# Retention and a softplus MLP on one core: one PSUM group for scores, state and values, and three smaller moves

## The chip, the core and the metric

The kernel runs on one core of one Trainium2 chip. The metric is the device time of one execution in microseconds (us); lower is better. The engines are named as in the profile: PE is TensorE (PEld its weight loads), ACT is ScalarE, DVE is VectorE, POOL is GpSimd, SP is the engine that issues the DMAs. Each engine runs its own instructions in order, and they wait for one another by semaphores.

## The reference

For 8 batches, 8 heads, 576 positions and head size 64 the attention part is a retention: `scores = q k^T / 8`, multiplied by a decay `gamma_h ** (i - j)` for `i >= j` and 0 above the diagonal, times `v`. Its output, 4608 tokens by 512, goes through an MLP:

```python
h = x @ w_in                                            # 512 -> 2048
g = np.maximum(h, 0.0) + np.log1p(np.exp(-np.abs(h)))   # softplus
return (g @ w_out).astype(np.float32)                   # 2048 -> 512
```

## The kernel before

**Attention.** The tokens are cut into 36 chunks of 128. A chunk's scores are masked, and what came before the chunk enters through a running state (one per batch and head) that is scaled on POOL. The first nine chunks run in plain fp32, two head pairs at once: a *double step* m (18 of them) handles half of a chunk. `scores_double` writes the scores and the new state of a double step into two PSUM banks (columns 0 to 3C of them, C = 128), `scores_double_out` masks the scores on DVE (two instructions, L176) and adds up the state (L185 or L187), `values_double` multiplies the masked scores and the earlier state into another pair of banks, and `values_double_out` brings the result into the MLP's input: a copy on ACT (L216) and the rounding remainder on DVE (L217). The other 27 chunks run in split fp32r steps, which the change does not touch.

**MLP.** 512 tokens are a unit u (9 units), 128 of the 2048 hidden features a part p (16). A *slot* i is one pair (u, p), 144 in all: `hidden_mm(i)` (L380, 12 matmuls of 512 columns, every operand split into a high and a low half), then on ACT three functions (`logs`, L389 to L391), on DVE the sum (`softplus`, L395), on ACT the cast of the high half and on DVE the low half (`softplus_split`, L399, L400), then `output_mm` (L413, 12 matmuls). On PE slot i runs `hidden_mm(i)` and then `output_mm(i - 1)`, so that the softplus of a slot has about one slot of time.

**Stages.** An opening runs the first nine double steps (m = 0 to 8, AHEAD = 9). Slots 0 to 18 (SPLIT = 19) then carry the other nine (m = 9 to 17), and in the same slots the MLP's weights are loaded and split, two pieces of 512 KB a slot, by `weight_step`, once at the head of the slot and once behind `softplus_split`: ACT `weight_a` (L443) and `weight_c` (L459), DVE half of `weight_a` (L445), `weight_d` (L464) and `weight_b` (L451), and the load of the piece two ahead, which waits until `weight_d` has freed a buffer. Before the change odd slots hold `scores_double(m)` and even slots `values_double(m)`:

```python
            if i % 2:
                scores_double(m, two_banks(2))
                scores_double_out(m)
                scale_next()
            else:
                values_double(m, two_banks(2))
                values_double_out(m)
                if i:
                    load_next()
            weight_step()
```

The order of instructions on every engine is that of the program; nothing reorders them. A tile's slot in a pool is handed on when all its readers are done. At the end of each unit `output_out` copies four results from PSUM (by turns ACT, L422, and DVE, L424) and stores them. PSUM holds four banks for y as two tiles of two banks each, two for the double steps, two that serve the opening and then h. The last slot takes its softplus in two halves of 256 columns.

Of the kernel before, what the change touches and what calls it, by code (L numbers as in the profile page):

```python
# [36 lines left out]
PIECE = 512  # L37
START_WEIGHTS = 3
# [21 lines left out]
def retention_softplus_ffn(ctx: ExitStack, tc, opening, first, others, w, dec, vsc, gchp, out):  # L60
# [7 lines left out]
    ps_y = ctx.enter_context(tc.tile_pool(name="ps_y", bufs=1, space=PSUM))  # L68
# [123 lines left out]
    def values_double(m, bank):  # L192
        L = live[-1 - m]
        start, _ = _chunk_kind(m // 2)
        n_cross = C if start is None else start
        if L["before"] is None:
            n_cross = 0
        for s in range(2):
            for h in range(2):
                rows = slice(h * D, (h + 1) * D)  # L200
                nc.tensor.matmul(bank[rows, s, 0:C], L["v"][:, s, rows], L["a"][:, h, s], start=True,  # L201
                                 stop=not n_cross, skip_group_check=True)
        if n_cross:
            for s in range(2):
                for h in range(2):
                    rows = slice(h * D, (h + 1) * D)
                    nc.tensor.matmul(bank[rows, s, 0:n_cross], L["before"][rows, s], L["q"][rows, s, 0:n_cross],  # L207
                                     start=False, stop=True, skip_group_check=True)
        L["o"] = bank

    def values_double_out(m):
        o = live.pop(-1 - m)["o"][:, :, 0:C]
        ch, pr = m // 2, 2 * (m % 2)
        xt = x_tile(ch // CPU)
        cols = slice((ch % CPU) * C, (ch % CPU + 1) * C)
        nc.scalar.copy(xt[:, HI, pr:pr + 2, cols], o)  # L216
        nc.vector.tensor_sub(xt[:, LO, pr:pr + 2, cols], o, xt[:, HI, pr:pr + 2, cols].bitcast(F32))  # L217
# [151 lines left out]
    hs = {}  # L369
# [3 lines left out]
    def hidden_mm(i):  # L373
        u, p = divmod(i, NF)
        xt = x_tile(u)
        h = later["ps_h"].tile([P, T], F32, tag="h", name="h")
        n = 0
        for a, b in TERMS:
            for kt in range(NKT):
                nc.tensor.matmul(h, ws[p][:, a, kt * P:(kt + 1) * P], xt[:, b, kt],  # L380
                                 start=(n == 0), stop=(n == 3 * NKT - 1))
                n += 1
        hs[i] = h

    def logs(i, cols=slice(0, T)):

        h = hs[i][:, cols]
# [6 lines left out]
    def softplus(i, ab, cols=slice(0, T)):  # L394
        nc.vector.scalar_tensor_tensor(ab, hs[i][:, cols], 0.0, ab, op0=ALU.max, op1=ALU.add)  # L395
# [7 lines left out]
    def output_mm(i):  # L403
        u, p = divmod(i, NF)
        parts = gs.pop(i)
        if p == 0:
            ys[u] = [ps_y.tile([P, 2, DM], F32, tag=f"y{n}", name=f"y{n}") for n in range(2)]
        for tt in range(CPU):
            y = ys[u][tt // 2][:, tt % 2]
            for n, (a, b) in enumerate(TERMS):  # L410
                g = parts[tt * len(parts) // CPU]
                at = tt % (CPU // len(parts)) * P
                nc.tensor.matmul(y, g[:, a, at:at + P], ws[p][:, b, PIECE:],  # L413
                                 start=(p == 0 and n == 0), stop=(p == NF - 1 and n == 2))

    def output_out(u, tt):

        y = ys[u][tt // 2][:, tt % 2]
        pool = later.get("osb", moe) if tt > 1 else moe
        osb = pool.tile([P, DM], F32, tag="osb", name="osb")  # L420
        if tt % 2 == 0:
# [60 lines left out]
    load_weight(0)  # L482
    for m in range(6):
        load_double(m)
    load_weight(1)
# [13 lines left out]
    def two_banks(n):  # L499
        pool, tag = ((ps_y, "y0"), (ps_y, "y1"), (ps_att, "bank"), (ps_open, "open"))[n]  # L500
# [8 lines left out]
    weight_a(0)  # L509
    weight_b(0)  # L510
    weight_c(0)
    weight_d(0)
    scale_values(0)
    for m in range(AHEAD):
# [9 lines left out]
        if m in (2, 4, 6):  # L524
            load_weight(m // 2 + 1)
        scale_values(m + 1)
        scores_double_out(m)
        if m in (4, 6):
            weight_b(m // 2 - 1)
        if m in (5, 7):  # L530
            weight_d(m // 2 - 1)
        if 0 < m < AHEAD - 1:
            values_double_out(m - 1)
        if m in (4, 6):
            weight_c(m // 2 - 1)
        if m in (3, 5):
            weight_a(m // 2)
        scale_next()
    wpos[0] = START_WEIGHTS
    open_pools.close()  # L540
    later["ps_h"] = ctx.enter_context(tc.tile_pool(name="ps_h", bufs=2, space=PSUM, side="right"))

# [3 lines left out]
    for i in range(NSLOT):  # L546
        j = i + LEAD
        if i < SPLIT:
            m = AHEAD + (i - 1) // 2
            if i % 2:  # L550
                scores_double(m, two_banks(2))
                scores_double_out(m)
                scale_next()
                if "raw" in later:
                    load_upto(NPLAIN + 1)
            else:
                values_double(m, two_banks(2))
                values_double_out(m)
                if i:
                    load_next()  # L560
# [34 lines left out]
        hidden_mm(i)  # L595
        ab = logs(i)
        if i < SPLIT:
            softplus(i, ab)
# [7 lines left out]
        if i >= SPLIT:  # L606
            softplus(i, ab)
# [9 lines left out]


    hidden_mm(i)
    halves = [slice(0, T // 2), slice(T // 2, T)]  # L620
    abs_ = [logs(i, cols) for cols in halves]
    output_mm(i - 1)
    gs[i] = []
    for ab, cols in zip(abs_, halves):
        softplus(i, ab, cols)
        gs[i].append(softplus_split(ab))
    output_mm(i)
    for tt in range(CPU):
        output_out(NUNIT - 1, tt)
# [53 lines left out]
```

## Time and profile before

| | us |
|---|---|
| median of 3 runs (lowest, highest) | 956.22 (955.93, 958.87) |
| the profiled execution | 956.29 |
| its span, first to last instruction | 954.6 |
| busy in the span: PE, ACT, DVE, POOL | 943.3, 674.6, 668.8, 280.0 |
| granted PE clock, mean | 0.999 of full speed |

The span is what the trace shows; the profiled execution's own time is 1.7 us longer, for what lies before and after it. PE is busy for 99% of the span, and the chain of work that ended last consists of PE for 96%. A row of the timeline gives start, duration, engine, source line, operation, the tile written and the tile read, and in square brackets the idle time of the engine ahead of it and what ended that. A row of the chain gives start, duration and what the chain was on; its pieces add up to the span.

### The profile page before, as it was taken

How to read it: one execution, taken by the hardware profiler on the slowest of the kernel's cores; microseconds unless marked ns; L12 is line 12 of the kernel's file. 1: busy time of each engine (PE TensorE's matmuls, PEld its weight loads, DVE VectorE, ACT ScalarE, POOL GpSimd, SP SyncE). 2: the span in 40 equal slices, each digit the busy share in tenths (PEclk: the TensorE clock that was granted, in tenths of full speed). 3: DMA queues.
4: the chain of work that ended last, by engine and by line, in shares of the span. 5: the costliest groups of instructions: out<-in, count | busy, mean ns of one | idle time of the engine just before them, and what ended most of it. 6: DMA issues, size and time to landing. Idle time of an engine off the chain costs nothing.

```text
span 954.6 us, 14474 instructions
## 1 busy us (share of the span) xinstructions
PE 943.3 (99%) x4934; PEld 788.5 (83%) x4934; DVE 668.8 (70%) x1507; ACT 674.6 (71%) x1449; POOL 280.0 (29%) x497
## 2 busy tenths in 40 slices
PE   7999999999999999999999999999999999999997
PEld 6777777888888888888888888888888888888886
DVE  6688855777877777777777787778777787753222
ACT  6677756777777777777777777777777777764443
POOL 5222112333343332333343333233333333200000
PEclk9999999999999999999999999999999999999999
DMA  8556623212312232213212222223212222201001
GB/s 316 180 162 214 196 92 105 65 52 67 98 63 67 59 102 67 67 51 99 78 50 67 67 94 67 67 56 105 67 52 64 78 85 66 67 1 45 1 1 44
DMA packets 28729, 79.85 MB, mean 84 GB/s; under 512 B 3440, under 2 KB 3440, under 8 KB 28656
## 3 DMA queue, kind: packets, MB, share of 16 engines
q1 hardware_dynamic: 28656, 78.93, 26.1%
q8 instruction: 39, 0.64, 0.3%
q14 instruction: 34, 0.28, 0.1%
HBM read 69.48 MB, written 9.44 MB: 83 GB/s over the span
## 4 chain that ended last, share of the span: by engine, by line
PE 96%; DMA 2%; ACT 1%; DVE 1%; POOL 0%; issue 0%; SPq 0%; POOLq 0%; ACTq 0%; DVEq 0%
PE h L380 41%; PE y L413 40%; PE os L348 7%; PE sc L266 3%; PE os L275 2%; DMA raw_rawp<-first 1%; PE bank L201 1%; PE bank L161 1%; PE bank L207 1%; DMA out<-osb 0%; PE bank L166 0%; DVE a L176 0%; ACT ab L390 0%; ACT ab L391 0%; ACT ab L389 0%; ACT osb L422 0%
## 5 line engine op out<-in xcount | busy, mean ns | idle before, releaser
L380 PE MATMUL h<-xt,w 128*128 128x512 f32 x1728 | 420.4, 392 | 0.0
L413 PE MATMUL y<-w,g 128*128 128x512 f32 x1728 | 415.8, 389 | 0.8 <-DVE g L400 0.8
L413 PEld LDWEIGHTS y<-w,g 128*128 128x128 f32 x1728 | 324.0, 188 | 69.6 <-DVE g L400 1.9
L380 PEld LDWEIGHTS h<-xt,w 128*128 128x128 f32 x1728 | 316.0, 188 | 62.6 <-issue 1.0
L241 POOL TENSOR_TENSOR raw<-raw,dec_sb 128x256 f32<-128x256 f32 x108 | 98.0, 908 | 436.3 <-DMA raw<-others 361.3
L400 DVE TENSOR_TENSOR g<-ab,g 128x512 fp32r<-128x512 f32 (+1 forms) x145 | 103.9, 716 | 98.8 <-ACT g L399 98.8
L399 ACT CAST g<-ab 128x512 fp32r<-128x512 f32 (+1 forms) x145 | 89.5, 617 | 114.4 <-DVE ab L395 114.4
L395 DVE SCALAR_TENSOR_TENSOR ab<-h,ab 128x512 f32<-128x512 f32 (+1 forms) x145 | 99.6, 687 | 82.4 <-ACT ab L391 76.6
L389 ACT ACTIVATE ab<-h 128x512 f32<-128x512 f32 (+1 forms) x145 | 86.2, 594 | 64.9 <-PE h L380 64.7
L391 ACT ACTIVATE ab<-ab 128x512 f32<-128x512 f32 (+1 forms) x145 | 91.3, 629 | 4.6
L390 ACT ACTIVATE ab<-ab 128x512 f32<-128x512 f32 (+1 forms) x145 | 91.2, 629 | 4.6
L255 ACT CAST hl<-raw 128x768 fp32r<-128x768 f32 x108 | 90.9, 841 | 1.7 <-POOL raw L246 1.7
L257 DVE TENSOR_TENSOR hl<-raw,hl 128x512 fp32r<-128x512 f32 x108 | 84.8, 785 | 1.5
L285 DVE TENSOR_TENSOR a<-sc,a 128x256 f32<-128x256 f32 x108 | 45.8, 424 | 55.9 <-ACT a L284 55.0
L361 ACT CAST xt<-os 64x128 fp32r<-64x128 f32 x216 | 56.3, 261 | 36.3 <-PE os L275 31.9
L348 PE MATMUL os<-ah,hl 128*128 128x256 f32 x324 | 73.3, 286 | 0.0
L365 DVE TENSOR_TENSOR xt<-os,xt 64x128 fp32r<-64x128 f32 x216 | 62.2, 288 | 2.8
L309 POOL TENSOR_TENSOR s<-s,gchp_sb 128x128 f32<-128x128 f32 x96 | 58.6, 611 | 9.2 <-DVE s L308 0.2
L317 ACT CAST ah<-a 128x256 fp32r<-128x256 f32 x108 | 44.0, 407 | 15.1 <-POOL a L286 10.9
L348 PEld LDWEIGHTS os<-ah,hl 128*128 128x128 f32 x324 | 53.6, 190 | 0.4
L286 POOL TENSOR_SCALAR_AFFINE_SELECT a<-a 128x256 f32<-128x256 f32 x108 | 44.9, 416 | 29.4 <-DVE a L285 28.5
L256 DVE TENSOR_TENSOR hl<-raw,hl 64x256 fp32r<-64x256 f32 x108 | 47.4, 439 | 8.5 <-ACT hl L255 5.5
(82 smaller groups left out, 786.5 us busy)
## 6 DMA issues: line engine op xcount, KB each, us to landing
raw<-others SPq DMA_DIRECT2D x108, 384.0 KB, 3.1
wst<-w SPq DMA_DIRECT2D x32, 512.0 KB, 3.7
out<-osb SPq DMA_DIRECT2D x36, 256.0 KB, 2.2
raw_rawp<-first SPq DMA_DIRECT2D x13, 512.0 KB, 4.6
raw_g<-first SPq DMA_DIRECT2D x3, 512.0 KB, 7.4
raw_ab<-first SPq DMA_DIRECT2D x2, 256.0 KB, 8.5
dec_sb<-dec SPq DMA_DIRECT2D x1, 512.0 KB, 3.9
part<-opening SPq DMA_DIRECT2D x1, 390.0 KB, 4.3
```

The source lines that it names most:

```text
L241: nc.gpsimd.tensor_mul(r[:, 2:4], r[:, 2:4], later["dec"][:, 2 * pr:2 * pr + 2])
L255: nc.scalar.copy(hl[:, 0:6], r)
L257: nc.vector.tensor_sub(hl[:, 6:10], r[:, 2:6], hl[:, 2:6].bitcast(F32))
L348: nc.tensor.matmul(o[:, :, 0:width], lhs, rhs, start=(n == 0), stop=(n == len(mms) - 1))
L380: nc.tensor.matmul(h, ws[p][:, a, kt * P:(kt + 1) * P], xt[:, b, kt], start=(n == 0), stop=(n == 3 * NKT - 1))
L389: nc.scalar.activation(ab, h, AF.Abs)
L390: nc.scalar.activation(ab, ab, AF.Exp, scale=-1.0)
L391: nc.scalar.activation(ab, ab, AF.Ln, bias=1.0)
L395: nc.vector.scalar_tensor_tensor(ab, hs[i][:, cols], 0.0, ab, op0=ALU.max, op1=ALU.add)
L399: nc.scalar.copy(g[:, HI], ab)
L400: nc.vector.tensor_sub(g[:, LO], ab, g[:, HI].bitcast(F32))
L413: nc.tensor.matmul(y, g[:, a, at:at + P], ws[p][:, b, PIECE:], start=(p == 0 and n == 0), stop=(p == NF - 1 and n == 2))
```

## The change

- In slots 1 to 17 the odd slot runs `scores_double(m)` and `values_double(m - 1)` one behind the other into the same two banks (the values in columns 3C to 4C, `VCOLS`), and both outputs behind them. The even slots have no attention any more, but for slot 18, which holds the last values. The load of the next double step moves to the odd slot, directly ahead of the scaling on POOL.
- The first piece of the weights is loaded behind the second double step instead of ahead of everything, and its conversion moves from ahead of the opening into it; the other pieces' steps shift by one or two iterations.
- The y tiles become four of one bank each, opened behind the opening; the opening's six banks are a pool of their own.
- At the end of unit 0 two of the four results are staged in the opening's input tiles `part0` and `part1` (free since the first double step) instead of two buffers shared with the masked scores.
- In the last slot `hidden_mm` is computed in two halves of 256 columns into two h tiles, and of the last four results the last is copied by ACT instead of DVE.

The core of the diff (left out are only the changed arguments of `logs` and `softplus`, which take the tile h instead of its number):

```diff
+VCOLS = slice(3 * C, 4 * C)
...
-    ps_y = ctx.enter_context(tc.tile_pool(name="ps_y", bufs=1, space=PSUM))
...
     def values_double(m, bank):
...
-                nc.tensor.matmul(bank[rows, s, 0:C], L["v"][:, s, rows], L["a"][:, h, s], start=True,
+                nc.tensor.matmul(bank[rows, s, VCOLS], L["v"][:, s, rows], L["a"][:, h, s], start=True,
...
     def values_double_out(m):
-        o = live.pop(-1 - m)["o"][:, :, 0:C]
+        o = live.pop(-1 - m)["o"][:, :, VCOLS]
...
-    def hidden_mm(i):
+    def hidden_mm(i, cols=slice(0, T)):
...
-                nc.tensor.matmul(h, ws[p][:, a, kt * P:(kt + 1) * P], xt[:, b, kt],
+                nc.tensor.matmul(h, ws[p][:, a, kt * P:(kt + 1) * P], xt[:, b, kt, cols],
...
     def output_mm(i):
-            ys[u] = [ps_y.tile([P, 2, DM], F32, tag=f"y{n}", name=f"y{n}") for n in range(2)]
+            ys[u] = [later["ps_y"].tile([P, DM], F32, tag=f"y{n}", name=f"y{n}") for n in range(CPU)]
...
-    def output_out(u, tt):
-        y = ys[u][tt // 2][:, tt % 2]
-        pool = later.get("osb", moe) if tt > 1 else moe
-        osb = pool.tile([P, DM], F32, tag="osb", name="osb")
-        if tt % 2 == 0:
+    def output_out(u, tt, last=0):
+        y = ys[u][tt]
+        if u == 0 and tt > 1:
+            osb = parts[tt - 2][:, 0:DM]
+        else:
+            osb = (later["osb"] if tt > 1 else moe).tile([P, DM], F32, tag="osb", name="osb")
+        if tt % 2 == last:
...
-    load_weight(0)
     for m in range(6):
         load_double(m)
-    load_weight(1)
+        if m in (2, 5):
+            load_weight(m // 3)
...
-        pool, tag = ((ps_y, "y0"), (ps_y, "y1"), (ps_att, "bank"), (ps_open, "open"))[n]
+        pool, tag = ((ps_open, "open0"), (ps_open, "open1"), (ps_att, "bank"), (ps_open, "open2"))[n]
...
-    weight_a(0)
-    weight_b(0)
-    weight_c(0)
-    weight_d(0)
     scale_values(0)
     for m in range(AHEAD):
...
-        if m in (2, 4, 6):
-            load_weight(m // 2 + 1)
+        if m in (3, 5, 7):
+            load_weight((m + 1) // 2)
         scale_values(m + 1)
         scores_double_out(m)
-        if m in (4, 6):
+        if m in (2, 4, 7):
             weight_b(m // 2 - 1)
-        if m in (5, 7):
-            weight_d(m // 2 - 1)
+        if m in (3, 5):
+            weight_d((m - 3) // 2)
         if 0 < m < AHEAD - 1:
             values_double_out(m - 1)
-        if m in (4, 6):
+        if m in (2, 4, 7):
             weight_c(m // 2 - 1)
-        if m in (3, 5):
-            weight_a(m // 2)
+        if m in (1, 3, 6):
+            weight_a(m // 3)
         scale_next()
+    weight_d(START_WEIGHTS - 1)
...
             if i % 2:
-                scores_double(m, two_banks(2))
+                bank = two_banks(2)
+                scores_double(m, bank)
+                values_double(m - 1, bank)
                 scores_double_out(m)
+                values_double_out(m - 1)
+                if i > 1:
+                    load_next()
                 scale_next()
...
-            else:
+            elif i == SPLIT - 1:
                 values_double(m, two_banks(2))
                 values_double_out(m)
-                if i:
-                    load_next()
             weight_step()
...
-    hidden_mm(i)
-    halves = [slice(0, T // 2), slice(T // 2, T)]
-    abs_ = [logs(i, cols) for cols in halves]
+    hs = [hidden_mm(i, slice(n, n + T // 2)) for n in (0, T // 2)]
+    abs_ = [logs(h) for h in hs]
...
-        output_out(NUNIT - 1, tt)
+        output_out(NUNIT - 1, tt, last=1)
```

## Rows read from the trace of the kernel before

**Rows 1.** Timeline of the opening: start, duration, engine, line, operation, out<-in, [idle <-releaser].
```profile
11.05 1.06 ACT L153 ACTIVATE raw_g<-raw_g,part 128x64 f32<-128x64 f32 x4
11.76 0.73 POOL L137 TENSOR_TENSOR raw_g<-raw_g,part 128x256 f32<-128x256 f32 x1
...
21.38 0.71 PE L161 MATMUL bank<-raw_rawp 64*128 64x128 f32 x8 [0.56 <-POOL raw_rawp L137]
```
**Rows 2.** Chain of waits, end of the opening and first slots: start, duration, what.
```profile
22.48 0.44 PE bank L201 x8
...
25.32 0.43 PE bank L166 x8
...
27.61 2.96 PE h L380 x12
...
32.55 0.70 DVE ab L395
...
34.73 3.06 PE y L413 x12
```
**Rows 3.** Chain of waits, slots 7 and 8, the pattern of slots 1 to 16.
```profile
75.57 2.72 PE y L413 x12
78.29 0.59 PE bank L201 x8
78.88 0.58 PE bank L207 x8
79.46 2.95 PE h L380 x12
...
85.13 0.65 PE bank L161 x8
```
**Rows 4.** Timeline of DVE and of ACT in the same slots, the loop's marks.
```profile
72.70 0.69 DVE L395 SCALAR_TENSOR_TENSOR ab<-h,ab 128x512 f32<-128x512 f32 x1 [0.52 <-ACT ab L391]
...
77.09 0.28 DVE L185 TENSOR_TENSOR s<-bank,s 128x128 f32<-128x128 f32 x1
...
79.56 0.68 DVE L395 SCALAR_TENSOR_TENSOR ab<-h,ab 128x512 f32<-128x512 f32 x1
...
81.93 0.36 ACT L216 CAST xt<-bank 128x256 fp32r<-128x256 f32 x1
82.21 0.68 ACT L443 ACTIVATE wst<-wst 128x512 f32<-128x512 f32 x1
83.39 0.68 ACT L459 CAST w<-wst 128x512 fp32r<-128x512 f32 x1 [0.49 <-DVE wst L451]
...
85.91 0.69 DVE L395 SCALAR_TENSOR_TENSOR ab<-h,ab 128x512 f32<-128x512 f32 x1 [0.52 <-ACT ab L391]
```
**Rows 5.** One line's instructions in 40 to 130 us; durations in ns, minimum/median/maximum.
```profile
L451 DVE SCALAR_TENSOR_TENSOR wst<-wst x26: 680/686/1224, 42.1 to 126.0; 128x512 int32<-128x512 int32 x26
```
**Rows 6.** Loads of double steps (tile raw_rawp) in 40 to 130 us, from issue.
```profile
DMA to landing us min/median/max: 4.4/4.6/5.1
```
**Rows 7.** Timeline of DVE at the end of unit 0.
```profile
145.13 0.76 DVE L176 TENSOR_TENSOR a<-bank,mask 128x256 f32<-128x256 f32 x2 [1.13 <-DMA out<-osb]
```
**Rows 8.** Chain of waits, slots 18 to 20.
```profile
147.28 2.94 PE h L380 x12
...
152.94 0.23 PE sc L266 x2
...
153.41 2.75 PE h L380 x12
```
**Rows 9.** Timeline of the last 10 us.
```profile
944.99 0.42 DVE L395 SCALAR_TENSOR_TENSOR ab<-h,ab 128x256 f32<-128x256 f32 x1 [3.00 <-ACT ab L389]
...
946.67 3.05 PE L413 MATMUL y<-w,g 128*128 128x512 f32 x12 [0.58 <-DVE g L400]
...
948.99 0.69 DVE L424 COPY osb<-y 128x512 f32<-128x512 f32 x1 [1.08 <-ACT osb L422]
...
950.38 0.69 DVE L424 COPY osb<-y 128x512 f32<-128x512 f32 x1 [0.70 <-ACT osb L422]
```

More of the change, by code (lines that the diff above doesn't have):

```diff
@@ L206, in values_double @@
                     rows = slice(h * D, (h + 1) * D)
-                    nc.tensor.matmul(bank[rows, s, 0:n_cross], L["before"][rows, s], L["q"][rows, s, 0:n_cross],
+                    nc.tensor.matmul(bank[rows, s, 3 * C:3 * C + n_cross], L["before"][rows, s], L["q"][rows, s, 0:n_cross],
                                      start=False, stop=True, skip_group_check=True)
@@ L366, in value_out @@
         return rest
-    hs = {}
     gs = {}
     ys = {}
-    def hidden_mm(i):
+    def hidden_mm(i, cols=slice(0, T)):
         u, p = divmod(i, NF)
         xt = x_tile(u)
-        h = later["ps_h"].tile([P, T], F32, tag="h", name="h")
+        h = later["ps_h"].tile([P, T], F32, tag="h", name="h")[:, cols]
         n = 0
@@ L379, in hidden_mm, with logs @@
             for kt in range(NKT):
-                nc.tensor.matmul(h, ws[p][:, a, kt * P:(kt + 1) * P], xt[:, b, kt],
+                nc.tensor.matmul(h, ws[p][:, a, kt * P:(kt + 1) * P], xt[:, b, kt, cols],
                                  start=(n == 0), stop=(n == 3 * NKT - 1))
                 n += 1
-        hs[i] = h
-    def logs(i, cols=slice(0, T)):
-        h = hs[i][:, cols]
+        return h
+    def logs(h):
         ab = moe.tile([P, h.shape[1]], F32, tag="ab", name="ab")
@@ L392, in logs, with softplus @@
         return ab
-    def softplus(i, ab, cols=slice(0, T)):
-        nc.vector.scalar_tensor_tensor(ab, hs[i][:, cols], 0.0, ab, op0=ALU.max, op1=ALU.add)
+    def softplus(h, ab):
+        nc.vector.scalar_tensor_tensor(ab, h, 0.0, ab, op0=ALU.max, op1=ALU.add)
     def softplus_split(ab):
@@ L414, in output_mm @@
                                  start=(p == 0 and n == 0), stop=(p == NF - 1 and n == 2))
-    def output_out(u, tt):
-        y = ys[u][tt // 2][:, tt % 2]
-        pool = later.get("osb", moe) if tt > 1 else moe
-        osb = pool.tile([P, DM], F32, tag="osb", name="osb")
-        if tt % 2 == 0:
+    def output_out(u, tt, last=0):
+        y = ys[u][tt]
+        if u == 0 and tt > 1:
[3 more added lines that the diff above has]
+        if tt % 2 == last:
             nc.scalar.copy(osb, y)
@@ L541, in retention_softplus_ffn @@
     later["ps_h"] = ctx.enter_context(tc.tile_pool(name="ps_h", bufs=2, space=PSUM, side="right"))
+    later["ps_y"] = ctx.enter_context(tc.tile_pool(name="ps_y", bufs=1, space=PSUM, side="right"))
     SPLIT = NPLAIN - LEAD
@@ L594, in retention_softplus_ffn @@
             break
-        hidden_mm(i)
-        ab = logs(i)
+        h = hidden_mm(i)
+        ab = logs(h)
         if i < SPLIT:
-            softplus(i, ab)
+            softplus(h, ab)
             gs[i] = [softplus_split(ab)]
@@ L606, in retention_softplus_ffn @@
         if i >= SPLIT:
-            softplus(i, ab)
+            softplus(h, ab)
             if ends:
@@ L616, in retention_softplus_ffn @@
             output_out(i // NF - 1, 3)
-    hidden_mm(i)
-    halves = [slice(0, T // 2), slice(T // 2, T)]
-    abs_ = [logs(i, cols) for cols in halves]
+    hs = [hidden_mm(i, slice(n, n + T // 2)) for n in (0, T // 2)]
+    abs_ = [logs(h) for h in hs]
     output_mm(i - 1)
     gs[i] = []
-    for ab, cols in zip(abs_, halves):
-        softplus(i, ab, cols)
+    for h, ab in zip(hs, abs_):
+        softplus(h, ab)
         gs[i].append(softplus_split(ab))
```

## The prediction, made before the changed kernel ran

> **What bounds the kernel now.** I read the chain of waits first. In slots 1 to 16 it is PE alone, piece behind piece: 2.72 us of output matmuls, 0.59 and 0.58 for the values, 2.95 hidden matmuls, and in the next slot 0.65 for the scores [rows 3]. With 0.43 for a state [rows 2] two slots take 0.59 + 0.58 + 0.65 + 0.43 + 2 x (2.95 + 2.72) = 13.59 us. From slot 20 on a hidden group that doesn't follow fp32 attention takes 2.75 [rows 8].
>
> PE alone says little about what comes next, so I read the timelines of ACT and DVE in the same slots. Call S(i) the start of softplus(i) on DVE; 34.73 - 32.55 = 2.18 us after it PE may start the output matmuls of slot i [rows 2]. S runs 72.70, 79.56, 85.91 for slots 6, 7, 8: 6.86 us from even to odd, 6.35 from odd to even, 13.21 a pair [rows 4]. None of these softplus waits for PE: two wait for ACT's functions, the third comes straight behind other DVE work. Weight conversion and softplus are thus a loop of ACT and DVE with its own pace, only 0.38 us a pair faster than PE. Whatever makes PE faster there meets this loop at once, and what lengthens it by more than 0.38 slows the kernel.
>
> **The slots on PE.** The merged block is 0.65 + 0.43 + 0.44 + 0.58 = 2.10 us; the 0.44 is a values group behind a state group [rows 2]. The even slot's hidden group then follows output matmuls and takes 2.75. A pair needs 2.10 + 2.95 + 2.72 + 2.75 + 2.72 = 13.24 us, 0.35 less than now.
>
> **The slots on ACT and DVE.** The same instructions run, but the copy of the values (L216) now stands in the odd slot behind `scores_double_out`, and it reads the very two banks that DVE's masks and state read. What do two engines do that read one PSUM tile? Rows 9 show it twice, at the end of the kernel. A softplus half starts at 944.99 and was released by ACT's read of the other half of its h tile, not by its own input. DVE's copy at 948.99 waited 1.08 us for ACT's copy out of the same y tile. So readers of one tile take turns in program order, even at other columns. In both cases ACT is first; the change needs the other order, which no row shows. The Trainium skill (PSUM — Partial Sum Buffer, section PSUM bank collisions raise a hardware error) says that software must order any two engines on one bank and the same partitions, two reads included, whichever comes first. By that rule the copy waits for DVE's state instruction, as I take it below; without such an order the time is that of the second rival.
>
> Price of this wait. In slot 7 the state ends at 77.09 + 0.28 = 77.37 [rows 4]. ACT is strict in order: behind the copy stand `weight_a`, `weight_c` and the three softplus functions. The copy's record lasts 0.36 us and the next instruction starts 0.28 behind its start, so I count `weight_a` (0.68) as 0.60; from `weight_c` to softplus it is 85.91 - 83.39 = 2.52 [rows 4]. 77.37 + 0.28 + 0.60 + 2.52 = 80.77, that is 8.07 us behind S(6), where it is 6.86 now. From odd to even the copy's absence gives nothing: `weight_c` waits 0.49 us for DVE there anyway [rows 4], so 6.35 stays. A pair of the loop takes 14.42 us. I take 14.5, because the scaling on POOL now runs beside the odd softplus chain: an instruction such as L451 takes 0.69 us alone and up to 1.22 beside POOL [rows 5]. Two such in the chain make at most 2 x 0.54; little of it seems likely, since POOL has 0.73 us an instruction alone [rows 1] and falls partly on other work. Bounds: 14.2 (the masks and state begin a little sooner) and 15.5. PE with its 13.24 then idles about 1.2 us a pair.
>
> **The moved load.** The load of a double step goes from the even slot to the odd one; on SP it stays between the two weight loads, and its buffer was freed by PE long before. POOL's scaling now stands directly behind it and waits for it. It is issued before the state instruction at the latest, lands 5.1 us later at most [rows 6], which is 77.09 + 5.1 - 80.77 = 1.4 us behind the odd softplus, and two scalings of 0.73 [rows 1], 1.2 at worst, end 3.8 behind it. PE wants them with the next odd block, 2.18 + 2.72 = 4.9 behind it. On POOL only the next odd slot's state is queued behind. So no cost; if the cover of 1.1 us went, the scores would wait.
>
> **The opening.** Three pieces bring the first hidden group forward from 27.61 [rows 2]. The values of double step 8 no longer stand before it: 27.61 - 25.75 = 1.86 us, 25.75 being the end of the last state group [rows 2]. The fourth double step's data were there by 11.05, when ACT used them without waiting, but POOL scaled them at 11.76, held up by a chain that starts with the second double step's load [rows 1]; with 512 KB less ahead of that load the 0.71 goes. PE's wait of 0.56 at 21.38 for a later load [rows 1] goes too, as the third weight piece is now queued behind that load. The weight conversion that moves into the opening (three DVE and two ACT instructions) lies under PE's fp32 work; if it did not, DVE's part costs up to 3 x 0.69. Bounds of the three pieces: 1.86 and 3.7. I take 3.13: hidden(0) at 24.48, S(0) 4.94 later [rows 2] at 29.42.
>
> **The sum to slot 18.** S(1) = 29.42 + 8.07 = 37.49, PE being ahead of it or catching up within a pair. S(13) = 37.49 + 6 x 14.5 = 124.49, and the output matmuls of slot 13 start at 126.67. Behind slot 14 the weights are done and PE is the bound again. To hidden(18) it still has 2.72; slot 15 with 0.65 + 0.44 + 0.58 = 1.67 (no state in the last chunk) + 2.95 + 2.72; slot 16 with 2.75 + 2.72; slot 17 with 1.67 + 2.95 + 2.72; and 1.17 of values: 24.04. So hidden(18) starts at 150.71 instead of 147.28 [rows 8]: 3.43 us later. At the end of unit 0 DVE's wait of 1.13 us for a store [rows 7] goes with the extra staging tiles. A new one comes: the second staging copy takes the buffer of masked scores that PE reads in slot 17, 1.67 us on; behind it on DVE stand one more copy and the masks, and PE needs them only after its hidden group of 2.95. That hides it.
>
> **Slots 19 to 142** are fp32r attention and the MLP; nothing in them changes but the size of the y tiles, for which PE does not wait. I count nothing.
>
> **The tail.** The last hidden group becomes 24 matmuls of 256 columns at 0.23 / 2 us [rows 8], 2.76 us instead of 2.75, and its first half is ready 1.38 us sooner. So PE's 0.58 us wait for g [rows 9] goes (0 to 0.58). Behind PE's end at 946.67 + 3.05 = 949.72 two copies stand in a row now, to 951.07, because they share a y tile [rows 9]; with one tile each only one of at most 0.69 + 0.03 is left: 0.63 less. Together 1.2 us.
>
> **Sum.** 3.43 - 1.2 = +2.2 us on the profiled execution's 956.29, which is 0.07 above the median of the runs: **958.5 us**. A change of 0.3%, 2.9 us, is about what a measurement of this kernel can tell from none.
>
> **Rivals.**
> - *POOL beside the loop* (slower). If the scaling on POOL falls on L400, L464 and L451 of the odd chain, a pair grows by one or two times 0.54. Above 14.6 us a pair the kernel is more than 0.3% slower; at 14.96 it is 958.5 + 6 x 0.46 = 961.3, at 15.5 it is 964.5. For it: such durations occur now, under `weight_d` and `weight_b` of the odd slot [rows 5]. Against: POOL's work then meets fewer such instructions. [...]
> - *The copy doesn't wait for DVE's reads* (faster). Even to odd is then 6.86 plus 0.36 for the remainder at most, a pair at most 13.6 and more likely PE's 13.24. S(1) is at 36.6, six pairs of 13.3 lead to 126.67 - 8.1 = 118.6, hidden(18) is at 142.6, 4.7 earlier than before, and the time 956.29 - 4.7 - 1.2 = 950.4. For it: no row shows DVE first and ACT second. Against it are the two cases of rows 9.
> - *The opening doesn't move* but for the 1.86: 1.3 later, 959.8. That the dropped DMA piece isn't what delays it is the case here.
>
> **How the numbers follow.** Forecast 62%, of which a seventh lies above +0.3%; POOL beside the loop 20%; copy without a wait 9%; the opening stuck 9%. Faster by over 0.3%: 9%. Slower: 62 / 7 = 9, plus 20, plus 6 of the last: 35%. Within: 56%. The range is that of the forecast with its bounds, 14.2 us a pair and a better opening below (958.5 - 1.8 - 0.6 = 956.1), the POOL rival at its middle above, and a little of the others: 955.8 to 961.6.
>
> **What would show it.** In the changed trace: ACT's L216 released by DVE's L185 in the odd slots; softplus 8.1 and 6.35 us apart by turns; PE idle about 1.2 us a pair ahead of L413 (by L400) or L380 (by L464); hidden(0) near 24.5 and hidden(18) near 150.7; no idle PE ahead of the last L413. Wrong would be a pair of 13.3 us or of 15 and more.

## The result and the profile after

The changed kernel takes 960.64 us (median of 7 runs, 960.02 to 961.30) beside 956.74 (955.91 to 958.87) for the kernel before on the same chip: a ratio of 1.0032, with a 95% interval of 1.0021 to 1.0042. It is slower, by about the bound of 0.3%. The seven times of the kernel before fall into two groups, 955.9 to 956.7 and 958.2 to 958.9 us (see the last section): the change costs 4 to 5 us beside the first and about 2 beside the second. The profiled execution took 960.02 us with a span of 958.3, against 956.29 and 954.6 before. In the page's chain of work that ended last PE's share falls from 96% to 87%; ACT has 7% and DVE 5% now.

**The loop of ACT and DVE.** Timeline of DVE and ACT in the slots 6 to 8; the columns are those of [rows 4], and two lines that stood there come back here in their new order.

```profile
74.33 0.69 DVE L394 SCALAR_TENSOR_TENSOR ab<-h,ab 128x512 f32<-128x512 f32 x1 [0.53 <-ACT ab L390]
...
78.72 0.28 DVE L185 TENSOR_TENSOR s<-bank,s 128x128 f32<-128x128 f32 x1
...
79.09 0.37 ACT L216 CAST xt<-bank 128x256 fp32r<-128x256 f32 x1 [2.28 <-DVE s L185]
...
82.45 0.69 DVE L394 SCALAR_TENSOR_TENSOR ab<-h,ab 128x512 f32<-128x512 f32 x1 [0.53 <-ACT ab L390]
...
88.80 0.69 DVE L394 SCALAR_TENSOR_TENSOR ab<-h,ab 128x512 f32<-128x512 f32 x1 [0.52 <-ACT ab L390]
```

ACT is ready for the copy of the values (L216) 2.28 us before it runs, and it runs when DVE has read the state out of the same two banks (78.72 + 0.28 = 79.00). Softplus now runs 8.12 and 6.35 us apart by turns, where [rows 4] have 6.86 and 6.35. From S(1) = 38.96 to S(13) = 125.90 six pairs take 86.94 us, 14.49 each. The view of waits (ACT, 30 to 140 us; columns: total us, times, longest) shows the same wait at every copy:

```profile
ACT xt L216 <- DVE s L185: 13.7, 6, 2.3
...
ACT xt L216 <- DVE s L187: 2.3, 1, 2.3
ACT xt L216 <- DVE a L176: 1.5, 1, 1.5
```

**The end of the opening.** Timeline of PE, to be read beside [rows 2]:

```profile
23.53 0.71 PE L161 MATMUL bank<-raw_g 64*128 64x128 f32 x8
24.17 0.45 PE L166 MATMUL bank<-raw_g 128*64 128x64 f32 x8
25.80 2.98 PE L380 MATMUL h<-xt,w 128*128 128x512 f32 x12 [1.17 <-DVE s L187]
```

The values of double step 8 are gone from here, but the first hidden group waits 1.17 us for DVE's state instruction of that double step. In the chain the work between the output matmuls of slot 13 and hidden(18), which was at 147.28 before [rows 8], reads:

```profile
128.18 3.02 PE y L412 x12
...
131.84 0.59 PE bank L201 x8
...
144.76 0.59 PE bank L201 x8
...
152.77 2.95 PE h L380 x12
```

**The tail.** Timeline of the last 10 us, to be read beside [rows 9]: the last two output groups (24 matmuls) now follow one another without the wait of 0.58 us, and one copy ends 0.62 us behind PE's end at 948.28 + 5.63 = 953.91, where it was 1.35.

```profile
948.28 5.63 PE L412 MATMUL y<-w,g 128*128 128x512 f32 x24
...
953.95 0.58 ACT L423 COPY osb<-y 128x512 f32<-128x512 f32 x1 [0.77 <-PE y L412]
```

On PE's timeline the last hidden group starts 4.92 us later than before (945.41 against 940.49) and the span ends 3.7 later.

### The profile page after: what moved, and what is told of

Same layout as the page of the kernel before. It is cut to its first block, busy times and chain, and to the rows that moved or that the text cites. A ratio compares the mean times of both kernels' runs of the same rounds, so it can differ in the third digit from the quotient of the medians.

```text
span 958.3 us, 14519 instructions
## 1 busy us (share of the span) xinstructions
PE 942.6 (98%) x4946; PEld 788.0 (82%) x4946; DVE 661.7 (69%) x1507; ACT 675.8 (71%) x1449; POOL 272.2 (28%) x497
## 3 DMA queue, kind: packets, MB, share of 16 engines
HBM read 69.48 MB, written 9.44 MB: 82 GB/s over the span
## 4 chain that ended last, share of the span: by engine, by line
PE 87%; ACT 7%; DVE 5%; DMA 1%; issue 0%; POOL 0%; ACTq 0%; SPq 0%; DVEq 0%
PE h L380 37%; PE y L412 37%; PE os L348 6%; PE sc L266 3%; PE os L275 2%; ACT w L460 1%; DVE ab L394 1%; DVE wst L452 1%; ACT wst L444 1%; ACT ab L389 1%; ACT ab L390 1%; DVE w L465 1%; ACT g L398 1%; ACT ab L388 1%; DVE a L176 1%; DMA raw_rawp<-first 1%
## 5 line engine op out<-in xcount | busy, mean ns | idle before, releaser
L380 PE MATMUL h<-xt,w 128*128 128x512 f32 (+1 forms) x1740 | 420.3, 390 | 5.8 <-DVE w L465 4.6
L399 DVE TENSOR_TENSOR g<-ab,g 128x512 fp32r<-128x512 f32 (+1 forms) x145 | 101.2, 698 | 96.7 <-ACT g L398 96.7
```

Source lines behind the costliest of these rows:

```text
L399: nc.vector.tensor_sub(g[:, LO], ab, g[:, HI].bitcast(F32))
```

## Experiments

All runs, with the ratio to the kernel before on the same chip, and the marks that the profiled executions show. A pair is the distance of softplus over two slots, a mean over the steady part. In the kernel before and in e2 softplus catches up with PE and waits for it now and then (7.45 us from slot 4 to 5 in the kernel before, instead of 6.87), so the 13.21 of one pair is not the pace; for these two the pair is that of PE's hidden groups. hidden(0) and hidden(18) are from PE's timeline, where the kernel before has 27.54, 147.21 and a pair of 13.57.

| label | median us | ratio (95%) | pair | hidden(0) | hidden(18) |
|---|---|---|---|---|---|
| changed kernel | 960.64 | 1.0032 (1.0021 to 1.0042) | 14.49 | 25.80 | 152.70 |
| e1_values_out_first | 955.49 | 0.9979 (0.9968 to 0.9990) | 13.79 | 27.53 | 148.70 |
| e2_not_merged | 952.47 | 0.9948 (0.9933 to 0.9963) | 13.56 | 26.76 | 145.59 |
| e3_merge_only | 964.24 | 1.0068 (1.0053 to 1.0083) | 14.5 | 27.97 | 155.61 |
| e4_first_and_own_pool | 953.42 | 0.9956 (0.9942 to 0.9970) | 13.79 | 25.04 | 146.22 |
| e5_own_pool | 959.02 | 1.0010 (1.0001 to 1.0020) | 14.48 | 27.92 | 154.87 |
| e6_no_scaling | 951.79 | 0.9934 (0.9915 to 0.9953) | 13.01 | 24.49 | 142.56 |
| e7_load_later | 977.69 | 1.0208 (1.0188 to 1.0228) | 18.6 | 25.26 | 172.34 |
| e8_two_bank_y | 961.03 | 1.0035 (1.0021 to 1.0049) | 14.48 | 26.27 | 153.24 |
| e9_scaling_gated | 955.60 | 0.9984 (0.9974 to 0.9995) | 14.05 | 24.15 | 148.06 |
| e10_own_pool_again | 958.98 | 1.0017 (1.0009 to 1.0026) | 14.48 | 25.69 | 152.49 |
| e11_gate_at_d | 954.29 | 0.9964 (0.9950 to 0.9977) | 13.70 | 24.48 | 146.59 |
| e12_gate_at_a | 951.77 | 0.9932 (0.9919 to 0.9944) | 13.35 | 25.06 | 144.70 |

### The merge alone, and everything but the merge

`e3_merge_only` is the kernel before with the first part of the change alone; `e2_not_merged` is the changed kernel with the attention of the double steps spread over two slots again:

```diff
             if i % 2:
-                bank = two_banks(2)
-                scores_double(m, bank)
-                values_double(m - 1, bank)
+                scores_double(m, two_banks(2))
                 scores_double_out(m)
-                values_double_out(m - 1)
-                if i > 1:
-                    load_next()
                 scale_next()
...
-            elif i == SPLIT - 1:
+            else:
                 values_double(m, two_banks(2))
                 values_double_out(m)
+                if i:
+                    load_next()
```

> The kernel before with the merge alone: scores, state and values of slots 1 to 17 in one bank pair in the odd slot, the load of a double step there too; opening, y tiles, staging and tail as before. Theory: pairs of softplus 14.5 us apart; hidden(0) near 26.8 since the values of double step 8 no longer stand ahead of it; hidden(18) near 154.8 instead of 147.3, so about 964 us (962.5 to 965.5). Rival (the merge is neutral or gains and the loss is elsewhere): 953 to 957.

> The changed kernel with the attention of slots 0 to 18 as it was before: scores in odd slots, values in even slots, each with the bank pair for itself, and the load of a double step in the even slot. All other parts of the change stay. Theory (the merge costs, the rest gains): the pair is PE's 13.57 us again; the opening brings 1.1 us, the end of unit 0 0.6, the unit ends 0.6 and the tail 1.2, so about 952.8 us (952 to 954). Rival (the cost sits in another part, the opening or the y tiles): 957 or more.

Both times came out as expected, 964.24 and 952.47, and so did the pairs, 14.5 and 13.56; hidden(0) of e3 came at 27.97 instead of 26.8, in an execution with a mean granted clock of 0.995. The merge costs 6.5 us alone (1.0068) and about 8 with the rest (1.0032 against 0.9948); the rest of the change gains about 5. So the change is two changes of opposite sign, and the version without the merge is faster than either kernel.

### The copy's wait

`e1_values_out_first` turns the two outputs of the merged block round, so that ACT copies the values before DVE reads scores and state:

```diff
+                values_double_out(m - 1)
                 scores_double_out(m)
-                values_double_out(m - 1)
```

> The changed kernel with one swap in the odd slots: values_double_out(m - 1) stands ahead of scores_double_out(m), so that ACT's copy of the values comes first among the readers of the bank pair and DVE's masks second. The same instructions run in the same slots. Theory (ACT's copy waits for DVE's reads of the same tile and holds back the weight steps and softplus behind it): the copy runs when PE has written the values, from even to odd softplus takes about 6.5 us instead of 8.1, a pair becomes PE's own 13.24 us instead of 14.49, PE's idle time in slots 3 to 13 goes, hidden(18) starts near 143.3 instead of 152.8, and the profiled execution takes about 950.6 us (949.5 to 953). Rival (the merged slot as such is too much for ACT and DVE, whatever the order in it): the pair stays above 14 us and the time at 958 or more.

Half of the expectation held. ACT's L216 no longer waits for DVE, and 5 us go: 955.49. That the wait was DVE's reading of the same banks is shown by this, and by e2, where the copy has a bank pair of its own and doesn't wait either. Hidden(0) was 1.73 us later here than in the changed kernel, in an opening that the edit doesn't touch; from there to hidden(18) it took 121.17 us instead of 126.90. But a pair took 13.79 and not 13.24: even to odd 6.66 us, odd to even 7.13 where it had been 6.35. The timeline of POOL, DVE and ACT behind the softplus of slot 7 (80.57) shows why:

```profile
82.15 1.08 POOL L137 TENSOR_TENSOR raw_rawp<-raw_rawp,part 128x256 f32<-128x256 f32 x1 [2.65 <-DMA raw_rawp<-first]
...
82.54 0.97 DVE L446 TENSOR_SCALAR wst<-wst 128x512 int32<-128x512 uint32 x1
...
83.44 1.10 DVE L465 TENSOR_TENSOR w<-wst,w 128x512 fp32r<-128x512 f32 x1
...
85.17 0.67 ACT L460 CAST w<-wst 128x512 fp32r<-128x512 f32 x1 [0.92 <-DVE wst L452]
```

DVE's weight instructions, 0.42 and 0.69 us alone, take 0.97 and 1.10 beside POOL, and ACT waits for what follows. In the changed kernel the same POOL work (82.73 to 84.04 there) fell on softplus at 82.45 and DVE's gap behind it, and stretched at most the low half of g (L399, 0.69 to 0.92 us), because the copy's wait had put softplus later: one wait covered the other.

### The first hidden group and the closed pool

The banks of h were last used by double step 7, and yet hidden(0) waits for double step 8. The opening's six banks are one pool in the changed kernel, closed as a whole. `e5_own_pool` gives the pair of banks that h takes over a pool of its own:

```diff
+    ps_odd = open_pools.enter_context(tc.tile_pool(name="ps_odd", bufs=1, space=PSUM, side="right"))
...
-        pool, tag = ((ps_open, "open0"), (ps_open, "open1"), (ps_att, "bank"), (ps_open, "open2"))[n]
+        pool, tag = ((ps_open, "open0"), (ps_odd, "open1"), (ps_att, "bank"), (ps_open, "open2"))[n]
```

> The changed kernel with one edit: the opening's second pair of banks (open1) gets a pool of its own. My theory of the opening: the first hidden group waits 1.17 us for the state instruction of double step 8 because the h tiles take over a whole closed pool, although their banks (open1) were last used by double step 7. Then with open1 in its own pool that wait goes: hidden(0) starts at about 24.7 instead of 25.80, all the slots behind it keep their pace (14.5 us a pair), and the time is about 1.1 us below the changed kernel's, 2.0 us above before (ratio about 1.002). Rival: the wait belongs to something else that ends with the state, such as the last values written to the MLP's input; then hidden(0) stays near 25.8 and the time at +3.1 us.

The time fell as expected or somewhat more: a ratio of 1.0010 instead of 1.0032. But in the execution profiled TensorE ran at half its clock for a part of the opening (last section), so its hidden(0) says nothing, and the kernel was run again:

> The changed kernel with open1 in a pool of its own once more, for a trace at full granted clock (in the execution profiled before, TensorE's clock was 0.50 from 9 to 15 us of the opening). If the closed pool is what hidden(0) waits for in the changed kernel, hidden(0) starts at about 24.7 without a wait for DVE's state instruction, hidden(18) about 1.1 us sooner than at 152.77, and the time is 1 to 2 us below the changed kernel's 960.6. Otherwise hidden(0) stays near 25.8.

Timeline of PE in that run:

```profile
25.31 0.45 PE L167 MATMUL bank<-raw_g 128*64 128x64 f32 x8
25.69 3.06 PE L381 MATMUL h<-xt,w 128*128 128x512 f32 x12
```

The wait is gone: hidden(0) follows the state group at once. The other traces agree: all eight kernels with this pool apart show no wait there, and the three merged kernels that close the six banks as one pool (changed, e1, e8) show 1.17 us each. So the cause is shown. The start, 25.69, is not the expected 24.7, and hidden(18) comes 0.21 us sooner instead of 1.1, because in this execution PE reached the scores of double step 8 at 24.66 instead of 23.53; counted from these scores, hidden(18) comes 1.34 us sooner (127.83 and 129.17). The opening varies by 1 to 2 us between executions with the loads that it waits for. The medians of the two runs, 959.0 both, are 1.6 us below the changed kernel's, on other chips. `e4_first_and_own_pool` has both edits:

> The swap of the run before it, and the opening's odd score banks (those that h takes over) in a pool of their own. Theory (hidden(0) waits 1.17 us for the state of double step 8, though that lies in other banks, because the h tiles take over a whole closed pool): with the pool apart hidden(0) starts near 24.7 instead of 25.8, and the time is 0.8 to 1.2 us below that of the swap alone. Rival (hidden(0) waits for something else on DVE, the remainder of double step 7 above all): hidden(0) stays at 25.6 to 25.8 and the time the same.

It took 953.42 us, 2.1 below e1 on the same chip, more than the 0.8 to 1.2 expected. PE's timeline has hidden(0) at 25.04 without a wait.

### POOL beside the loop

> The run with values first and a pool of its own for open1, with POOL's scaling of double steps 9 to 17 left out (part of the computation is missing: two multiplications per double step). Theory A, POOL beside the loop: the odd-to-even part of a pair is 7.12 us there because DVE's weight instructions take 0.97 and 1.10 us instead of 0.42 and 0.69 beside POOL. Without POOL's work a pair goes from 13.79 to PE's 13.24, six and a half pairs give 3.5 us: about 950 us (ratio to before about 0.992). Theory B, the DMA: the moved load stands between the weight loads, a weight piece lands 0.63 us late for ACT, and a pair stays at 13.6 or more: 952.5 to 953.5 us.

```diff
-        nc.gpsimd.tensor_mul(L["q"], L["q"], decp_sb[half])
+        if m < AHEAD:
+            nc.gpsimd.tensor_mul(L["q"], L["q"], decp_sb[half])
...
-        if m >= AHEAD:
-            v, f = value_scale(m)
-            nc.gpsimd.tensor_mul(v, v, f.unsqueeze(2).broadcast_to([P, 4, D]))
```

Theory A holds. The profiled execution took 949.71 us (the fastest of four, the median is 951.79), and its timelines of DVE and PE give softplus a pace of 13.01 us a pair and hidden groups one of 13.15 (two slots apart):

```profile
69.41 0.69 DVE L393 SCALAR_TENSOR_TENSOR ab<-h,ab 128x512 f32<-128x512 f32 x1 [0.53 <-ACT ab L389]
76.07 0.68 DVE L393 SCALAR_TENSOR_TENSOR ab<-h,ab 128x512 f32<-128x512 f32 x1
82.42 0.69 DVE L393 SCALAR_TENSOR_TENSOR ab<-h,ab 128x512 f32<-128x512 f32 x1 [0.53 <-ACT ab L389]
```

```profile
70.42 3.01 PE L379 MATMUL h<-xt,w 128*128 128x512 f32 x12
...
83.57 3.01 PE L379 MATMUL h<-xt,w 128*128 128x512 f32 x12
```

So PE is the bound of the merged slots once the copy's wait and POOL's work are away, at 13.15 us; the prediction's sum of PE's rows was 13.24. Theory B is out by the same trace: ACT still waits for the weight piece behind the odd softplus, and the pair loses nothing by it. DVE and ACT in that slot:

```profile
78.05 0.42 DVE L445 TENSOR_SCALAR wst<-wst 128x512 int32<-128x512 uint32 x1
78.56 0.69 DVE L464 TENSOR_TENSOR w<-wst,w 128x512 fp32r<-128x512 f32 x1
...
79.09 0.69 ACT L443 ACTIVATE wst<-wst 128x512 f32<-128x512 f32 x1 [0.56 <-DMA wst<-w]
```

### The place of the load

> The run with values first and a pool of its own for open1, with the load and the scaling of the next double step moved in the odd slot from behind the attention to behind the second weight step, so that two weight loads go ahead of it. Theory A (POOL beside the loop): the scaling lands some 3 us later, beside other DVE weight instructions; those become the ones that are stretched, and a pair stays between 13.5 and 13.9 us, 952 to 954 us. Theory B (the weight piece that lands late): ACT's wait of 0.63 us for a weight piece goes, a pair falls to about 13.2 to 13.3, and the time to about 950.5 us.

```diff
-                if i > 1:
-                    load_next()
-                scale_next()
...
             gs[i] = [softplus_split(ab)]
             weight_step()
+            if i % 2:
+                if i > 1:
+                    load_next()
+                scale_next()
```

It took 977.69 us, some 24 above e4, which no theory foresaw. The timeline of SP, POOL and PE of one slot:

```profile
61.59 11.86 SPq L439 DMA_DIRECT2D wst<-w  x3
73.54 0.38 SPq L122 DMA_DIRECT2D raw_rawp<-first  x1
...
78.05 0.85 POOL L138 TENSOR_TENSOR raw_rawp<-raw_rawp,part 128x256 f32<-128x256 f32 x1 [11.66 <-DMA raw_rawp<-first]
...
78.96 0.72 PE L162 MATMUL bank<-raw_rawp 64*128 64x128 f32 x8 [2.90 <-POOL raw_rawp L138]
```

SP issues in order, and its second weight load of the slot waits until `weight_d` has freed a buffer. Moved behind it, the load of the double step left 3.65 us behind the odd softplus (69.89 in that slot), where e4 issues it 3.01 ahead of it (60.71 and 63.72). PE then waits for the scaled q in the odd slots from 5 to 13, and in those stretches its granted clock falls: from 76 to 80 us PE is busy for 1.07 of 4 us, from 80 to 82 the granted clock is 0.50 (1.2 GHz, the lower level), and from 84 on it is 1.00 again after work without a gap. The two theories could not be told apart with this; e6 did it.

### When POOL runs

`e9_scaling_gated` starts POOL's scaling at a chosen time: in the even slot it stands behind a one-column POOL instruction that reads what a DVE weight instruction at the head of that slot writes. e11 and e12 differ only in what it reads.

```diff
             weight_step()
+            if i and i % 2 == 0:
+                if wpos[0] - 1 in wl:
+                    last = wl[wpos[0] - 1][:, 0:1, 1].bitcast(F32)
+                    nc.gpsimd.tensor_mul(gate, last, last)
+                scale_next()
```

In e11 it reads `weight_dst(wpos[0] - 2)[1][:, 0:1]`, in e12 `wl[wpos[0] - 1][:, 0:1, 0]`.

> The run with values first and a pool of its own for open1, with POOL's scaling of the next double step moved from the odd slot to the even one, behind a one-column POOL instruction that reads what DVE's weight_b at the head of the even slot wrote; so it starts when DVE has no weight instruction left ahead of softplus and runs beside DVE's two idle gaps (0.52 and 0.69 us) and softplus, which reads PSUM. All work is done. Theory (what POOL costs is which DVE instruction it meets): DVE's weight instructions keep 0.42 and 0.69 us, a pair takes 13.15 us as in the run without scaling instead of 13.79, hidden(18) starts about 3 us sooner than at 146.2, and the time is about 950.5 us (ratio to before about 0.993), below every kernel so far. Rival (POOL's work costs DVE or ACT the same wherever it stands): a pair stays at 13.7 to 13.9 and the time at about 953.5.

DVE's weight instructions did keep 0.42 and 0.69 us, but the scaling was now too late for PE (timeline of POOL and PE, slot 7):

```profile
69.35 0.20 POOL L568 TENSOR_TENSOR gate<-wst 128x1 f32<-128x1 f32 x1 [7.92 <-DVE wst L454]
69.49 0.73 POOL L139 TENSOR_TENSOR raw_rawp<-raw_rawp,part 128x256 f32<-128x256 f32 x1
...
70.27 0.72 PE L163 MATMUL bank<-raw_rawp 64*128 64x128 f32 x8 [0.72 <-POOL raw_rawp L139]
```

One wait took the other's place: 14.05 us a pair, 955.60 us. I had looked only at DVE's gaps and not at when PE asks, 69.39 in this slot. The two that followed, on one chip:

> The run with the scaling behind a one-column POOL instruction in the even slot, with that instruction now reading what weight_d at the head of the even slot writes instead of weight_b, so that POOL starts about 0.7 us sooner. All work is done. In the earlier run PE waited for the scaled q: 0.72 us and more in every odd slot, and a pair took 13.94 us. Theory: POOL's first instruction now meets weight_b of the same step and stretches it by about 0.5 us, but softplus waits 0.53 us for ACT there, so this is hidden; PE's wait falls to 0 to 0.2 us, a pair to 13.15 to 13.35 and the time to 951 to 952 us (ratio to before about 0.994). Rival: the meeting delays softplus after all, a pair stays at 13.6 or more, 953.5 to 955 us.

> The same with the one-column POOL instruction reading what DVE's half of weight_a at the head of the even slot writes, some 1.6 us sooner than behind weight_b. Theory: POOL is done before PE asks, but now two DVE weight instructions (weight_d and weight_b) are stretched by 0.4 and 0.5 us, more than the 0.53 us that softplus waits for ACT: softplus comes about 0.4 us later, a pair takes 13.5 to 13.6 us and the time is 1.5 to 2.5 us above the run with the instruction behind weight_d. Rival: only PE's wait counts, and both runs take the same time within 0.5 us.

I had them the wrong way round: e11 took 954.29 us, e12 951.77. In e11 the gate itself was held up. Timeline of DVE and POOL:

```profile
68.75 0.68 DVE L454 SCALAR_TENSOR_TENSOR wst<-wst 128x512 int32<-128x512 int32 x1
...
68.97 0.51 POOL L568 TENSOR_TENSOR gate<-w 128x1 f32<-128x1 f32 x1 [7.13 <-DVE w L467]
69.44 0.73 POOL L139 TENSOR_TENSOR raw_rawp<-raw_rawp,part 128x256 f32<-128x256 f32 x1
```

A one-column instruction that takes 0.20 us in e9 took 0.51 and ended with DVE's instruction, at 69.48 and 69.43; the scaling started 0.15 us ahead of PE's asking (69.59 in this slot), where in e9 it started 0.10 behind it, and PE still waited 0.47 us instead of 0.72. In e12 POOL was first, and DVE was stretched:

```profile
68.14 0.19 POOL L568 TENSOR_TENSOR gate<-wst 128x1 f32<-128x1 f32 x1 [5.34 <-DVE wst L448]
68.29 0.74 POOL L139 TENSOR_TENSOR raw_rawp<-raw_rawp,part 128x256 f32<-128x256 f32 x1
...
68.41 1.17 DVE L467 TENSOR_TENSOR w<-wst,w 128x512 fp32r<-128x512 f32 x1 [0.40 <-ACT w L462]
...
69.33 0.71 PE L163 MATMUL bank<-raw_rawp 64*128 64x128 f32 x8
69.50 1.10 DVE L454 SCALAR_TENSOR_TENSOR wst<-wst 128x512 int32<-128x512 int32 x1
```

PE didn't wait for q, and about 0.1 us for the second scaling (1.07 us beside DVE's L454 instead of 0.62). Of the 0.90 us by which the two were stretched 0.61 lay in the gap ahead of softplus: odd to even took 6.64 us instead of 6.35, and a pair 13.3, but for one odd slot in which PE waited for POOL again. This is the fastest of the kernels that do all the work: 0.9932 (0.9919 to 0.9944) of the kernel before, on one chip beside 958.34. Against e2, on another chip, its lead is within the intervals. Hidden(0) starts 1.70 us sooner than in e2, and from there to hidden(18) it needs 119.64 us, e2 118.83; but e2 has the values of double step 8 ahead of hidden(0), e12 behind it. Counted from the scores of double step 8, the same work takes 120.66 us in e12 and 121.77 in e2: by these two traces, the merge done this well gains 1.1 us over attention spread on two slots.

### The y tiles

> The changed kernel with the y tiles as two tiles of two banks, as before the change. By my sum for the tail the two copies behind PE's end share a y tile again: +0.63 us there. By my reading of the slots behind the attention's change, five unit ends gain 0.1 us each with one-bank tiles (0.57 us up to slot 143), so these go too: together +1.2 us on the changed kernel's time, ratio to before about 1.0045. Rival: the gain at the unit ends comes from the staging tiles or from chance; then only +0.6.

```diff
-            ys[u] = [later["ps_y"].tile([P, DM], F32, tag=f"y{n}", name=f"y{n}") for n in range(CPU)]
+            pairs = [later["ps_y"].tile([P, 2, DM], F32, tag=f"y{n}", name=f"y{n}") for n in range(2)]
+            ys[u] = [pairs[n // 2][:, n % 2] for n in range(CPU)]
```

Timeline of the last 8 us:

```profile
948.98 5.63 PE L413 MATMUL y<-w,g 128*128 128x512 f32 x24
...
955.37 0.59 ACT L424 COPY osb<-y 128x512 f32<-128x512 f32 x1 [0.77 <-DVE osb L426]
```

The last copy ends 1.35 us behind PE again (955.96 and 954.61), as in the kernel before; one-bank tiles are worth 0.73. The time, 0.4 us above the changed kernel's, agrees with the rival. The gain at the unit ends went only in part: from slot 18 to slot 143 the distance to the kernel before shrinks by 0.41 us, in the changed kernel by 0.56. The timelines of ACT and DVE at the end of a unit (around hidden(113), 763.18 before and 768.23 in the changed kernel) show what the y tiles do there. In the kernel before:

```profile
762.30 0.59 ACT L422 COPY osb<-y 128x512 f32<-128x512 f32 x1 [0.32 <-PE y L413]
...
763.44 1.28 DVE L400 TENSOR_TENSOR g<-ab,g 128x512 fp32r<-128x512 f32 x1 [0.58 <-ACT g L399]
```

In the changed kernel:

```profile
768.07 0.69 DVE L399 TENSOR_TENSOR g<-ab,g 128x512 fp32r<-128x512 f32 x1 [0.16 <-ACT g L398]
```

With two banks in a tile, ACT's copy of the third result waits 0.32 us until PE has written the fourth into the same tile; the low half of g follows 0.42 us later, beside POOL's scaling, and takes 1.28 us. DVE then comes 0.9 us later to the masked scores (L318) that PE's next values read, and PE's slot takes 6.67 us instead of 6.54. ACT's wait stands at each of the six unit ends from slot 33 to slot 113 in the kernels with two-bank tiles (before, e3, e8) and at none in the changed kernel, e2 and e10, where g takes 0.69 and the slot 6.54 each time. Where POOL starts behind g (one of the six ends in the kernel before and in e8, two in e3), g keeps its 0.69 in those kernels too. So what the wait costs PE depends on when POOL works: 0.59 us in all in the kernel before, 0.15 in e8, 0.11 in e3.

## Why the prediction was near, and where it was off

958.5 us was forecast, 960.64 came, inside the range. The sign is the forecast's, the size is not: +2.2 us against +3.73 on the profiled executions.

**The slots on ACT and DVE: right.** L216 waits for L185, softplus runs 8.12 and 6.35 us apart (8.07 and 6.35 forecast), a pair takes 14.49 (14.5), and e1 shows that this order of reads is the cause. The rule of the Trainium skill (PSUM — Partial Sum Buffer, section PSUM bank collisions raise a hardware error), that two reads of a bank have to be ordered too, agrees with L216's waits for L185 and L187, seven of up to 2.3 us.

**The slots on PE: right, though nothing in the changed kernel shows it.** PE idles there for L465 and for L399. Only e6 reaches PE's own pace, 13.15 us (13.24).

**The moved load: right.** It costs nothing where it stands: POOL is done by 84.04, and PE takes the scaled data at 87.59. e7 shows how much hangs on the place that the prediction named, between the two weight loads.

**The opening: the step that failed.** It counted three pieces, 3.13 us, and hidden(0) at 24.48. The pieces ahead of the last scores came to 24.60 - 23.53 = 1.07 us instead of 1.27. Of the 1.86 for the values of double step 8 only 0.67 came (27.54 - 25.80 = 1.74, less 1.07): it was taken whole, as though nothing else stood behind them, where the runs showed the wait of 1.17 us for the state of double step 8. What is late next could have been asked: h is a tile in a pool that opens on the banks of another, and the diff moves that pool's border. Hidden(0) started at 25.80, softplus at 30.82 instead of 29.42, and S(13) at 125.90 instead of 124.49: the 1.4 us went through the loop unchanged.

**To slot 18: off by 0.6.** 24.04 us were counted from the output matmuls of slot 13 to hidden(18), 24.59 came (128.18 to 152.77). The row for values behind a state group, 0.44, was used for slots 15 and 17, where no state group stands ahead; there the first half takes 0.59 (131.84 and 144.76 in the chain), 0.30 more in all. And the output group of slot 13, which starts behind a wait, takes 3.0 us (128.18 to 131.19) instead of the 2.72 of one without: 0.29 more.

**Slots 19 to 142: a term put at nothing that was 0.57.** The distance to the kernel before falls from 5.49 to 4.92 us, by 0.09 to 0.15 at each of five unit ends. The prediction's reason was that PE doesn't wait for the y tiles. ACT does wait, in the kernel before, and with POOL's work in the way that delay reached PE (the traces of the y tiles, above).

**The tail: right, the exact sum partly by luck.** 1.2 us were counted, 4.92 - 3.7 = 1.2 came. The two parts were each larger: from the start of the last hidden group to PE's end 8.50 us instead of 9.23, 0.73 where 0.58 was counted, and the copies 0.73 where it was 0.63. From the last copy's end to the end of the span it took 3.8 us instead of 3.5, which nobody had counted.

So the errors are +1.4 in the opening and +0.6 ahead of slot 18, and -0.57 in the middle. Of the rivals, POOL beside the loop was right as a mechanism and wrong about this kernel: it is there in e1 and e4 with 0.64 us a pair (13.79 against 13.15 in e6), but in the changed kernel the copy's wait hides it. The prediction left DVE's `weight_a` out of what POOL can stretch. The Trainium skill (SBUF — State Buffer, section Who interferes with whom) names, beside instructions with two inputs in SBUF, `tensor_scalar` in its two-port modes; L446 at 0.97 us instead of 0.42 agrees. Its saying that the engine that issues first has the port and the other is blocked agrees with e11 and e12: in e11 the one-column gate waits for DVE's end, and in e12 POOL's 0.74 us stay whole while DVE's instruction is the longer.

## What to carry to other kernels

When one engine's reads of a PSUM tile are put behind another's, ask what is queued behind the second reader; here the order of two outputs in the program decided over 5 us, and the cheaper order had ACT first, whose queue was the longer. Before a wait is taken away, look at what its length has been hiding: behind the copy's wait stood POOL's work beside DVE's weight instructions, behind that the time at which PE asks. In these kernels the first tile of a new pool waited for the last users of the whole old pool, not of its own banks, so a pool's border is a dependency like any other.

## What the runs showed of the hardware

**TensorE's clock in the opening.** The first 20 us do not run alike in all executions. Windows of 2 us of the profiled execution of e5 (columns: window, its length, PE busy and its instructions, granted clock, DMA share, GB/s):

```profile
6.00:8.00 2.00, 0.68 (x14) 1.00 0.93 360
8.00:10.00 2.00, 1.18 (x10) 0.60 1.03 420
10.00:12.00 2.00, 2.00 (x22) 0.50 1.02 390
...
14.00:16.00 2.00, 2.00 (x26) 0.69 0.43 103
16.00:18.00 2.00, 2.00 (x36) 1.00 0.61 205
```

PE had waited 2.14 us for a load, then ran at half speed (1.2 GHz); it was busy without a gap from 8.82 on and was back at the full level in the window from 16. The wait alone doesn't decide: e7's profiled execution waited 2.30 us at the same place (until 8.74) and kept the full clock. That execution of e5 took 962.19 us, the ten others 958.4 to 959.8. The kernel before likely meets this more often: of its 23 runs beside e9 those with a mean granted clock of 0.999 and above took 955.5 to 958.1 us (7 runs), those of 0.997 and below 957.8 to 958.8 (12 runs), while of the changed kernel's 7 runs six are at 0.999 and above. Where in the kernel the clock of those runs was low no trace shows. So a part of the gain that e2's ratio shows, 5 us where the traces sum up to 3.3, is likely the fuller opening; that was not tried by itself.

**POOL and DVE.** The two hold each other up, and who is first decides: a POOL instruction of one column took 0.51 us instead of 0.20 behind DVE's, and DVE's took 1.17 instead of 0.69 behind POOL's. Softplus, which reads PSUM, kept its 0.69 us beside POOL (six times in the changed kernel between 40 and 130 us).
